# Four PSUM banks instead of two for the up steps of a fused retention and feed-forward kernel, and one pair of terms in another order

## Chip, cores and metric

The kernel runs on one core of one Trainium2 chip. The metric is the device time of one execution in microseconds (us). The span of a profile is about 1.8 us shorter than the time of the same execution.

The profiles name the engines: PE does the matmuls, PEld is its loading of weights, ACT does the gelu, DVE and POOL do elementwise work. POOL also issues most loads, and SP issues the transposes by DMA and the stores.

## The reference

Two stages follow one another. The first is a causal linear attention with decay (retention), 8 batches, 8 heads, 576 positions, head size 64. The second is a feed-forward block on all 4608 tokens.

```python
scores = (q @ k.T) / sqrt(64)                       # per batch and head
ret    = scores * gamma[h] ** (i - j)  (i >= j, else 0)
x      = (ret @ v), heads side by side              # 4608 x 512
h      = x @ w_in                                   # 512 -> 2048
out    = (h * sigmoid(1.702 * h)) @ w_out           # 2048 -> 512
```

## The kernel before

Tokens go in units of 128 rows (36 units) and chunks of 4 units (9 chunks). PSUM has eight banks, by name: H0 and H1 for the feed-forward matmuls, O0 and O1 for the outputs of the attention ("values" and "inter" terms), S0 to S3 for scores and states.

Every feed-forward matmul is issued as two 64-column halves, which run side by side (in the profile they start 3 or 4 ns apart). An "up" step makes one 128 x 512 tile of h in one bank with four such pairs; then ACT takes the bank through the gelu into SBUF. Up steps take turns on H0 and H1:

```python
def mm(y, lhs, rhs, reads, bank, start, stop=True, **kw):
    for r in HALVES:                                   # columns 0-63, 64-127
        op("pe", lambda e, r=r: e.matmul(y[r], lhs[:, r], rhs, ...),
           reads=reads, writes=[bank])
...
def up(c, f):
    bank = f"H{count['up'] % 2}"
    count["up"] += 1
    hb = banks[bank].ap()
    for a in range(HP):                                # 4 pairs of matmuls
        mm(hb, w_in_sb[:, a, P * f : P * f + P], xT[c % 3][:, a, :], [...],
           bank, a == 0, a == HP - 1)
    op("act", lambda e: e.activation(gT[c % 2][:, f, :], hb, AF.Gelu_apprx_sigmoid),
       reads=[bank], writes=[f"gT{c % 2}_{f}"])
```

The recording helper `op` turns these reads and writes into semaphore waits: the first weight load of an up step waits until the gelu that last read its bank has ended.

A phase is 16 up steps of one chunk, or the 16 "down" steps of one chunk. The attention of two coming units (a "block") is played after one step of each phase, in the whole phases after step 13 counted from 0. From the whole phases on only the block uses O0 and O1, until the last down phase; between blocks they lie idle.

```python
def block(m):                       # units a = 2m, b = 2m + 1
    inter(a); inter(b)              # state times q, into O0, O1
    scores(a + 2); scores(b + 2)    # needs the transposed q, k of units a+2, b+2
    scores_out(a + 2, 0)
    values(a); values(b)            # masked scores times v, into O0, O1
    values_out(a); values_out(b)    # DVE: O0, O1 -> xT
    ...
```

Before the first up phase the first four units are worked off one by one (the "head" of the run). For unit 3 the inter term is first, which needs the state that ACT copies for unit 2:

```python
        head_k(2, "act")            # state of unit 2, copied by ACT
        ...
        inter(3)
        values(3)
        values_out(3)
        ...
        play(16, lambda f: up(0, f), {9: [lambda: head_in(4, "dve")], ...})
```

`head_in(4)` transposes k and q of unit 4 on PE after step 9 of the first up phase; it needs their loads.

## Time and profile before

| | before |
|---|---|
| time, median of 3 (range) | 306.97 us (306.8 to 308.05) |
| span of the profile | 305.4 us |
| PE busy | 297.3 us (97%) |
| pace of a pair of 512-column matmuls | 0.216 us |
| an up step: four pairs on PE, one gelu on ACT | 0.8635 us without a loss, 0.597 us |

These lines are from the page of the profile before: engines, the chain that ended last, and groups of instructions (line, engine, operation, output and inputs, shape, count, then busy us, mean ns of one, idle us before it and what ended it).

```profile
span 305.4 us, 8273 instructions
PE 297.3 (97%) x3728; PEld 167.7 (55%) x3728; DVE 131.7 (43%) x277; ACT 121.4 (40%) x214; POOL 113.3 (37%) x139
...
PE 72%; DMA 15%; POOL 12%; issue 1%; DVE 0%; SPq 0%; POOLq 0%
...
L313 PE MATMUL psH<-xT,w_in_sb 128*64 128x512 bf16 (+1 forms) x1280 | 131.0, 359 | 0.1
L456 ACT ACTIVATE gT<-psH 128x512 bf16<-128x512 f32 x128 | 76.5, 597 | 49.6 <-PE psH L313 49.6
L313 PEld LDWEIGHTS psH<-xT,w_in_sb 128*64 128x64 bf16 x1280 | 63.1, 109 | 57.0 <-ACT gT L456 21.6
```

L313 is the helper `mm`, so groups are told apart by their tiles: `psH<-xT,w_in_sb` is an up step, `psH<-w_out_sb,gT` a down step. PE shows 0.1 us of idleness in up steps, and yet the weight loads (PEld) wait 21.6 us for the gelu.

The waits view of before, with the total, how often, and the longest:

```profile
engine line waited for: us in total, times, longest us
PEld psH L313 <- ACT gT L456: 23.5, 78, 0.3
```

Three stretches of the timeline view on PE before (start, duration, instruction, count, and in brackets the idle time before it). They are the end of the head, the wait for unit 4, and the block near 84 us:

```profile
start us, us, engine line op out<-in xcount [idle before <-releaser]
16.48 0.42 PE L432 MATMUL psO<-pm,vp 128*64 128x128 bf16 x8
16.70 0.42 PE L313 MATMUL psO<-qkT,kv 128*64 128x128 bf16 x8
17.53 0.41 PE L313 MATMUL psO<-qkT,kv 128*64 128x128 bf16 x8 [0.41 <-ACT kv L366]
17.78 0.39 PE L432 MATMUL psO<-pm,vp 128*64 128x128 bf16 x8
...
18.95 8.90 PE L313 MATMUL psH<-xT,w_in_sb 128*64 128x512 bf16 x80
...
28.24 0.41 PE L313 MATMUL psS<-ident,kq 128*64 128x128 bf16 x8 [0.16 <-DMA kq<-in_q_dram]
...
83.98 0.40 PE L413 MATMUL psS<-qkT 64*128 64x128 bf16 x8 [0.57 <-DMA qkT<-kq]
84.30 0.64 PE L432 MATMUL psO<-pm,vp 128*64 128x128 bf16 x16
```

At 17.53 us PE waits for ACT before the inter term of unit 3. At 28.24 us it waits for the q load of unit 4, and at 83.98 us for the transposed q and k of unit 13. After that last wait the chain that ended last holds PE alone, but for the last copy of an output on DVE (0.42 us). So the run has two parts: a start that DMA and POOL can hold up, until about 84 us, and some 221 us that only PE's own pace decides. I use the values of the block (84.30 us here, `psO<-pm,vp` x16) as the boundary: 305.36 - 84.30 = 221.06 us lie behind it.

### The profile page before, as it was taken

Reading aid. Unit: us, or ns where it says so; the run is one execution under the profiler, and the core shown is the slowest. Engines: PE = TensorE matmul, PEld = TensorE weight load, DVE = VectorE, ACT = ScalarE, POOL = GpSimd, SP = SyncE. Lnnn points to the kernel's source line nnn. Section 1 sums busy time; section 2 is a strip of 40 time slices with the busy share of each in tenths; the row PEclk is TensorE's granted clock in tenths of the full one; section 3 lists DMA queues with packets and bytes.
Section 4 is the critical chain, followed back from the end, with each engine's and each line's share of the span. In section 5 each row is a group of like instructions: output and inputs, shape, how many; then the busy total and the mean of one; then the engine's idle time right before and its main releaser. Section 6 shows DMA issues by size and latency. Waiting matters only on the chain.

```text
span 305.4 us, 8273 instructions
## 1 busy us (share of the span) xinstructions
PE 297.3 (97%) x3728; PEld 167.7 (55%) x3728; DVE 131.7 (43%) x277; ACT 121.4 (40%) x214; POOL 113.3 (37%) x139
## 2 busy tenths in 40 slices
PE   7789999999999999999999999999999999999996
PEld 3544699556554555455545554555455545554455
DVE  5681860418444464245444554426352635310000
ACT  8566346211146313631363126412651165116611
POOL 9799920745245464260328024600662000000000
PEclk9999999999999999999999999999999999999999
DMA  9999999999997999997699859894989420110022
GB/s 141 194 207 191 188 206 135 143 174 242 122 210 170 131 199 194 131 149 104 133 173 142 103 118 166 155 119 109 173 148 98 105 71 0 36 71 34 2 55 85
DMA packets 118131, 40.65 MB, mean 133 GB/s; under 512 B 107024, under 2 KB 111376, under 8 KB 118096
## 3 DMA queue, kind: packets, MB, share of 16 engines
q0 software_dynamic: 80016, 22.55, 68.4%
q1 hardware_dynamic: 38080, 17.57, 23.9%
q8 instruction: 29, 0.48, 0.7%
q14 instruction: 6, 0.05, 0.1%
HBM read 36.70 MB, written 9.44 MB: 151 GB/s over the span
## 4 chain that ended last, share of the span: by engine, by line
PE 72%; DMA 15%; POOL 12%; issue 1%; DVE 0%; SPq 0%; POOLq 0%
PE psH L313 60%; DMA kq<-in_q_dram 9%; POOL kq L203 6%; PE psS L313 4%; DMA qkT<-kq 3%; POOL vn L217 3%; PE psO L313 3%; PE psO L432 2%; DMA vn<-in_v_dram 2%; PE psS L413 2%; POOL vp L303 1%; POOL w_out_sb L232 1%; POOL w_in_sb L226 0%; POOL iota_c L238 0%; DVE osb L508 0%
## 5 line engine op out<-in xcount | busy, mean ns | idle before, releaser
L313 PE MATMUL psH<-xT,w_in_sb 128*64 128x512 bf16 (+1 forms) x1280 | 131.0, 359 | 0.1
L313 PE MATMUL psH<-w_out_sb,gT 128*64 128x512 bf16 x1024 | 115.5, 379 | 0.0
L456 ACT ACTIVATE gT<-psH 128x512 bf16<-128x512 f32 x128 | 76.5, 597 | 49.6 <-PE psH L313 49.6
L313 PEld LDWEIGHTS psH<-xT,w_in_sb 128*64 128x64 bf16 x1280 | 63.1, 109 | 57.0 <-ACT gT L456 21.6
L313 PEld LDWEIGHTS psH<-w_out_sb,gT 128*64 128x64 bf16 x1024 | 56.1, 110 | 48.6 <-ACT gT L456 1.9
L217 POOL DMA_DIRECT2D vn<-in_v_dram x39 | 33.6, 873 | 115.1 <-DMA qkT<-kq 115.1
L486 ACT ACTIVATE osb<-psH 128x512 f32<-128x512 f32 x32 | 19.1, 597 | 106.7 <-PE psH L313 106.7
L422 DVE TENSOR_TENSOR pm<-psS,mask 128x512 bf16<-128x512 f32 x64 | 41.3, 684 | 44.9 <-PE psS L413 44.9
L203 POOL DMA_DIRECT2D kq<-in_q_dram x39 | 34.4, 888 | 0.0
L203 POOL DMA_DIRECT2D kq<-in_k_dram x39 | 34.2, 883 | 0.0
L442 DVE TENSOR_TENSOR xT<-psO,gq 128x512 bf16<-128x512 f32 x36 | 23.5, 684 | 12.5 <-PE psO L432 12.0
L383 DVE TENSOR_TENSOR kvf<-psS,kvf 64x256 f32<-64x256 f32 x24 | 10.1, 422 | 25.4 <-PE psS L313 25.2
L303 DVE TENSOR_TENSOR vp<-vn,vfac 128x512 bf16<-128x512 f32 x29 | 18.8, 688 | 0.2
L381 DVE COPY kvf<-psS 64x256 f32<-64x256 f32 x12 | 5.1, 422 | 19.8 <-PE psS L313 19.7
L313 PEld LDWEIGHTS psS<-vp,kq 128*64 128x64 bf16 x256 | 10.3, 110 | 5.9 <-ACT kv L366 0.7
L413 PE MATMUL psS<-qkT 64*128 64x128 bf16 x288 | 12.2, 218 | 1.4 <-ACT qkT L338 0.7
L471 ACT ACTIVATE gT<-psH 128x512 bf16<-128x512 f32 x16 | 9.6, 597 | 8.4 <-PE psH L313 8.4
L313 PE MATMUL psS<-vp,kq 128*64 128x128 bf16 x256 | 12.6, 220 | 0.2 <-POOL vp L303 0.2
L508 DVE COPY osb<-psS 128x256 f32<-128x256 f32 x1 | 0.4, 425 | 28.5 <-PE psS L313 28.5
L432 PE MATMUL psO<-pm,vp 128*64 128x128 bf16 x288 | 12.0, 221 | 0.0
L389 DVE TENSOR_TENSOR kv<-psS,kvf 64x256 bf16<-64x256 f32 x12 | 5.1, 422 | 16.2 <-PE psS L313 16.1
L386 DVE CAST kv<-kvf 64x256 bf16<-64x256 f32 x36 | 11.4, 317 | 1.2
(52 smaller groups left out, 132.1 us busy)
## 6 DMA issues: line engine op xcount, KB each, us to landing
vn<-in_v_dram POOLq DMA_DIRECT2D x31, 256.0 KB, 5.3
out_dram<-osb SPq DMA_DIRECT2D x31, 256.0 KB, 2.4
kq<-in_k_dram POOLq DMA_DIRECT2D x31, 128.0 KB, 5.8
kq<-in_q_dram POOLq DMA_DIRECT2D x31, 128.0 KB, 5.9
w_in_sb<-in_moe_w_in_dram POOLq DMA_DIRECT2D x4, 512.0 KB, 9.9
w_out_sb<-in_moe_w_out_dram POOLq DMA_DIRECT2D x4, 512.0 KB, 14.6
out_dram<-osb SPq DMA_DIRECT2D x10, 128.0 KB, 2.4
vn<-in_v_dram POOLq DMA_DIRECT2D x8, 128.0 KB, 3.4
```

The source lines that it names most:

```text
L203: e.dma_start(kq[sl][p0 : p0 + n, i, :].rearrange("p (h d) -> p h d", d=DH), src[b, :, s0 : s0 + n, :].rearrange("h p d -> p h d"),)
L217: e.dma_start(vn[sl][p0 : p0 + n, :, :], v[b, :, s0 : s0 + n, :].rearrange("h p d -> p h d"),)
L303: op(eng, lambda e: e.tensor_tensor(vp[u % NVP].ap(), vn[sl].ap(), vfac[:, ty, :, None].to_broadcast([P, H, DH]), ALU.mult), reads=[f"vn{s ...
L313: op("pe", lambda e, r=r: e.matmul(y[r], lhs[:, r], rhs, start=start, stop=stop, skip_group_check=True, **kw), reads=reads, writes=[bank])
L383: op("dve", lambda e, d=acc, s=src: e.tensor_tensor(d, s, d, ALU.add), reads=[bank, kfk], writes=[kfk])
L386: op("dve", lambda e, d=dst, s=acc: e.tensor_copy(d, s), reads=[kfk, f"kv{kind}_{c}"], writes=[kvk])
L413: op("pe", lambda e, hp=hp, hh=hh, bank=bank: e.matmul(by_pair(bank)[:, hp, :], qt[64 * hh : 64 * hh + 64, hp, :], qt[64 * hh : 64 * hh + ...
L422: op("dve", lambda e: e.tensor_tensor(pm[u % 4][hh].ap(), by_pair(bank), m[:, None, :].to_broadcast([P, HP, P]), ALU.mult), reads=[bank, " ...
L432: op("pe", lambda e, hp=hp, hh=hh: e.matmul(ob[64 * hh : 64 * hh + 64, hp, :], vp[u % NVP][:, 2 * hp + hh, :], pm[u % 4][hh][:, hp, :], st ...
L442: op("dve", lambda e: e.tensor_tensor(xT[ch % 3][:, :, 128 * j : 128 * j + 128], by_pair(bank), gq[:, ty, :, :], ALU.mult), reads=[bank] + ...
L456: op("act", lambda e: e.activation(gT[c % 2][:, f, :], hb, AF.Gelu_apprx_sigmoid), reads=[bank], writes=[f"gT{c % 2}_{f}"])
L486: op("act", lambda e: e.activation(osb[o].ap(), y, AF.Copy), reads=[bank], writes=[f"osb{o}"])
```

## The change

The intent is to use O0 and O1 in the up steps while the attention does not need them, so that a bank's gelu has more time, and to fill PE's hole before the inter term of unit 3 with that unit's values.

```diff
--- before.py
+++ after.py
@@ -443,11 +443,7 @@
                 xT[ch % 3][:, :, 128 * j : 128 * j + 128], by_pair(bank), gq[:, ty, :, :], ALU.mult),
                reads=[bank] + [f"gq{i}_{ty}" for i in range(HP)], writes=[f"xT{ch % 3}_{j}"])
 
-        count = {"up": 0, "y": 0}
-
-        def up(c, f):
-            bank = f"H{count['up'] % 2}"
-            count["up"] += 1
+        def up(c, f, bank):
             hb = banks[bank].ap()
             for a in range(HP):
                 mm(hb, w_in_sb[:, a, P * f : P * f + P], xT[c % 3][:, a, :],
@@ -456,10 +452,8 @@
             op("act", lambda e: e.activation(gT[c % 2][:, f, :], hb, AF.Gelu_apprx_sigmoid),
                reads=[bank], writes=[f"gT{c % 2}_{f}"])
 
-        def up_half(c, i, half):
-
-            bank = f"H{count['up'] % 2}"
-            count["up"] += 1
+        def up_half(c, i, half, bank):
+
             hb = banks[bank].ap().rearrange("p (a b) -> p a b", b=256)
             n = slice(256 * half, 256 * half + 256)
             for j in range(2):
@@ -511,6 +505,10 @@
                 op("sp", lambda e, c0=c0, c1=c1: e.dma_start(
                     out[S * b + s0 : S * b + s0 + n, c0:c1], osb[r][:, c0:c1]),
                    reads=[f"osb{r}_{i}"], writes=[f"out{u}_{i}"], dma=f"d_last{i}")
+
+        def up_bank(i, n):
+
+            return ("H0", "O0", "H1", "O1")[i % 4] if i < n else ("H0", "H1")[i % 2]
 
         def warm(n):
 
@@ -666,8 +664,8 @@
         head_k(2, "act")
         head_v(2)
         setup_gelu()
-        inter(3)
-        values(3)
+        values(3, True)
+        inter(3, False)
         values_out(3)
         head_k(3, "act")
         setup_tail()
@@ -678,7 +676,7 @@
         scale_v(6, "pool")
         scale_v(7, "pool")
         warm(2)
-        play(16, lambda f: up(0, f), {
+        play(16, lambda f: up(0, f, up_bank(f, 8)), {
             9: [lambda: head_in(4, "dve")],
             11: [lambda: head_s(4)],
             12: [lambda: head_in(5, "dve")],
@@ -690,11 +688,11 @@
         warm(1)
         ready_t(4)
         fetch((8, 9), (10, 11), 8)
-        play(8, lambda i: up_half(1, i, 0), {
+        play(8, lambda i: up_half(1, i, 0, up_bank(i, 0)), {
             1: [lambda: head_vs(6)],
             5: [lambda: head_vs(7)],
         })
-        play(8, lambda i: up_half(1, i, 1), {})
+        play(8, lambda i: up_half(1, i, 1, up_bank(i, 8)), {})
         steps = [(down, 0), (down, 1)]
         for c in range(2, NCH):
             steps += [(up, c), (down, c)]
@@ -713,7 +711,7 @@
             events[p + 1, 9] = [lambda m=m: ready_v(m + 2)]
         for p, (step, c) in enumerate(steps[:-1]):
             if step is up:
-                play(16, lambda i: up(c, i), {i: events.get((p, i), []) for i in range(16)})
+                play(16, lambda i: up(c, i, up_bank(i, 12)), {i: events.get((p, i), []) for i in range(16)})
             else:
                 play(16, lambda i: down(c, i, ("H0", "H1")), {i: events.get((p, i), []) for i in range(16)})
         for r in (3, 0, 1):
```

In whole up phases steps 0 to 11 go round four banks and steps 12 to 15 stay on H0 and H1, since the block is played after step 13. In the first up phase it is the first eight steps, and in the half-width phase after it (`up_half`) the second half.

## The prediction

> **What bounds it.** TensorE. The busy line gives PE 297.3 of 305.4 us (97%), granted clock 0.999. From 84 us to the end the chain of waits is PE alone; before that it is POOL issues and DMA (DMA 15%, POOL 12%). In the timeline a pair of 512-column matmuls starts every 216 ns, so an up step of four pairs costs about 865 ns; its gelu takes 597 ns on ACT. So two banks are nearly enough: the waits view charges the gelu 23.5 us of weight-load idleness (78 waits), but mostly hidden. The gelu of step n-2 ends about 0.80 us after step n-1 starts and the weight load follows about 50 ns later. Weight loads that start 26 ns before their matmul cost nothing; one that starts 7 ns before delays the next pair (232 instead of 216 ns).
>
> The Trainium skill, "TensorE: Matmul & The Clock Gate" (queue depths), says TensorE can pull weight loads ahead of running matmuls. The trace agrees: unblocked loads start 214 ns ahead; those behind a bank wait do not.
>
> **What the change does.** No work is removed or added.
> 1. Up steps on four banks: step n waits for the gelu of step n-4, long done. Counting pair gaps of 229-233 ns after 84 us: 5, 6, 5, 5, 5, 5 and 8 in the seven whole up phases, 13-17 ns each, 0.60 us in all. Only the last phase keeps one (two banks in steps 12 to 15, no attention block between), so 0.59 us goes. The one such gap at the start of a down phase stays.
> 2. The first up phase has four such gaps in its first ten steps (0.06 us).
> 3. Unit 3: its inter term waits 0.41 us for the ACT copy of the state (17.53 us). Its values can run in that hole once POOL's scaled values are there (17.12 us), so the bank is done, and the first up step starts, about 0.2 us earlier (18.95 to 18.73).
>
> **Critical path.** Points 2 and 3 are swallowed: at 27.9 us PE waits (0.33 us over its pace) for unit 4's q load, set by POOL issues and DMA; that wait should grow to about 0.6 us. Anything left falls into the wait (0.73 us over pace) for a transposed qkT at 83.2 us, likewise on POOL and DMA. After 84 us no PE wait on a DMA shows and transposes land some 10 us early, so point 1's 0.59 us is real.
>
> The O banks add no wait: values_out (0.69 us on DVE) precedes the first up step on O0 by nearly three PE steps, and the next block comes two steps after the last gelu on O1.
>
> **Predicted:** 306.97 - 0.6 = 306.4 us; 305.6 to 307.3 with the run-to-run spread (306.8 to 308.05 before). Chances: faster by over 2% 0.01, within 2% 0.98, slower 0.01.
>
> **What would show it.** Right: weight-load waits on the gelu fall from 78 to some 25 or fewer; 232 ns gaps vanish from whole up phases, each about 0.08 us shorter; first up step about 0.2 us earlier but the waits near 28 and 83 us longer. Wrong: gaps of 232 ns remaining (cause not the bank), or the waits at 28 and 83 us not growing.
>
> **What would make it wrong.** The loads at 28 and 83 us landing earlier or later (up to 0.7 us either way); an unseen wait for the O banks before the block.

## More of the kernel before

The Trainium skill ("Trainium Kernel Development and Optimization", Performance Expectations) calls matmul busy time a bad metric for how close a kernel is to roofline, because matmuls are pipelined. In this trace, too, busy time misleads: a matmul whose weights come late is only recorded as longer (395 to 400 ns instead of 379), and the stall stays inside the 97%.

The timeline of the weight loads in an up phase, before:

```profile
88.22 0.57 PEld L313 LDWEIGHTS psH<-xT,w_in_sb 128*64 128x64 bf16 x8 [0.29 <-ACT gT L456]
89.10 0.57 PEld L313 LDWEIGHTS psH<-xT,w_in_sb 128*64 128x64 bf16 x8 [0.31 <-ACT gT L456]
```

Each step's eight weight loads come late and in a bunch, released by the gelu. The next view is PE's timeline in the last up phase, which has no block in it:

```profile
274.77 14.14 PE L313 MATMUL psH<-xT,w_in_sb 128*64 128x512 bf16 x128
288.74 7.07 PE L313 MATMUL psS<-w_out_sb,gT 128*64 128x512 bf16 x64
```

From the first matmul of this phase to the first of the next it takes 288.74 - 274.77 = 13.97 us for 16 steps, 0.873 us a step.

## The result, and the profile after

A ratio in this text is that of one kernel's runs to the other kernel's of the same job, with its 95% interval; it is not quite the ratio of the medians quoted beside it. A gap is the time from the start of the second half of one pair of matmuls to the start of the first half of the next pair.

| | before | after |
|---|---|---|
| time, median of 6 (range) | 306.92 us (306.49 to 308.05) | 306.28 us (305.69 to 307.0) |
| ratio, 95% interval | | 0.9977 (0.9955 to 0.9998) |
| span of the profile | 305.36 us | 304.22 us |
| values of the block near 84 us | 84.30 us | 83.90 us |
| from there to the end | 221.06 us | 220.32 us |
| gaps of 226 to 236 ns within up phases, after 84 us | 39 | 1 |

The difference is under 2%; the interval lies just below 1.

The page after:

```profile
span 304.2 us, 8276 instructions
PE 297.0 (98%) x3728; PEld 176.8 (58%) x3728; DVE 131.7 (43%) x277; ACT 121.3 (40%) x214; POOL 113.2 (37%) x139
...
L313 PEld LDWEIGHTS psH<-xT,w_in_sb 128*64 128x64 bf16 x848 | 47.0, 110 | 30.8 <-DVE xT L442 0.7
```

The waits view after:

```profile
PEld psH L313 <- ACT gT L452: 2.5, 8, 0.3
```

The gelu (now L452) holds weight loads 8 times instead of 78, and only two of the 8 are in up steps. In an up phase the loads now come one pair at a time (0.76 us for eight instead of 0.57) and wait for no gelu:

```profile
88.47 0.76 PEld L313 LDWEIGHTS psO<-xT,w_in_sb 128*64 128x64 bf16 x8
89.33 0.76 PEld L313 LDWEIGHTS psH<-xT,w_in_sb 128*64 128x64 bf16 x8
```

PE's timeline after, in the same stretches as before:

```profile
16.77 0.42 PE L432 MATMUL psO<-pm,vp 128*64 128x128 bf16 x8
17.00 0.42 PE L313 MATMUL psO<-qkT,kv 128*64 128x128 bf16 x8
17.56 0.41 PE L432 MATMUL psO<-pm,vp 128*64 128x128 bf16 x8
17.82 0.41 PE L313 MATMUL psO<-qkT,kv 128*64 128x128 bf16 x8
...
19.12 1.05 PE L313 MATMUL psH<-xT,w_in_sb 128*64 128x512 bf16 x8 [0.23 <-DVE maskc L279]
...
28.62 0.41 PE L313 MATMUL psS<-ident,kq 128*64 128x128 bf16 x8 [0.45 <-DMA kq<-in_q_dram]
...
83.35 0.62 PE L413 MATMUL psS<-qkT 64*128 64x128 bf16 x16
83.90 0.64 PE L432 MATMUL psO<-pm,vp 128*64 128x128 bf16 x16
...
273.75 1.03 PE L313 MATMUL psH<-xT,w_in_sb 128*64 128x512 bf16 x8
...
287.59 7.07 PE L313 MATMUL psS<-w_out_sb,gT 128*64 128x512 bf16 x64
```

The last up phase now takes 287.59 - 273.75 = 13.84 us, 0.865 us a step. Of the 1.14 us between the two spans, 0.74 us lie behind the boundary. The other 0.40 us lie ahead of it: the wait of 0.57 us for unit 13 is not there in this profile. Whether that is the change or chance is a question for the experiments.

The wait "DVE maskc" at 19.12 us is a name given by inference. The first up step waits for two things, xT and the first slice of w_in. xT was finished by DVE at 18.97 us and w_in landed at 18.99 us (18.64 us before), so the two were level.

### The profile page after: what moved, and what is told of

It is laid out like the page before. It is cut to its first block, busy times and chain, and to the rows that moved or that the text cites. A ratio compares the mean times of both kernels' runs of the same rounds, so it can differ in the third digit from the quotient of the medians.

```text
span 304.2 us, 8276 instructions
## 1 busy us (share of the span) xinstructions
PE 297.0 (98%) x3728; PEld 176.8 (58%) x3728; DVE 131.7 (43%) x277; ACT 121.3 (40%) x214; POOL 113.2 (37%) x139
## 4 chain that ended last, share of the span: by engine, by line
PE 89%; DMA 6%; POOL 3%; DVE 1%; issue 0%; POOLq 0%
PE psH L313 61%; PE psO L313 17%; PE psS L313 5%; DMA kq<-in_q_dram 3%; PE psS L413 3%; PE psO L432 3%; DMA vn<-in_v_dram 2%; POOL kq L203 2%; POOL vp L303 1%; DVE pm L422 0%; POOL w_in_sb L226 0%; DVE kv L368 0%; DVE qkT L327 0%; DVE xT L442 0%; POOL iota_c L238 0%
## 5 line engine op out<-in xcount | busy, mean ns | idle before, releaser
L313 PE MATMUL psH<-xT,w_in_sb 128*64 128x512 bf16 (+1 forms) x848 | 93.5, 355 | 0.2 <-DVE maskc L279 0.2
L313 PEld LDWEIGHTS psH<-xT,w_in_sb 128*64 128x64 bf16 x848 | 47.0, 110 | 30.8 <-DVE xT L442 0.7
L452 ACT ACTIVATE gT<-psH 128x512 bf16<-128x512 f32 x82 | 49.0, 597 | 35.4 <-PE psH L313 35.2
L313 PE MATMUL psO<-xT,w_in_sb 128*64 128x512 bf16 (+1 forms) x432 | 51.8, 363 | 0.0
L313 PEld LDWEIGHTS psO<-xT,w_in_sb 128*64 128x64 bf16 x432 | 24.6, 110 | 17.1
L452 ACT ACTIVATE gT<-psO 128x512 bf16<-128x512 f32 x46 | 27.5, 597 | 13.6 <-PE psO L313 13.6
L442 DVE TENSOR_TENSOR xT<-psO,gq 128x512 bf16<-128x512 f32 x36 | 23.4, 683 | 11.5 <-PE psO L432 10.9
```

The costliest lines, as they stand in the source:

```text
L313: op("pe", lambda e, r=r: e.matmul(y[r], lhs[:, r], rhs, start=start, stop=stop, skip_group_check=True, **kw), reads=reads, writes=[bank])
L442: op("dve", lambda e: e.tensor_tensor(xT[ch % 3][:, :, 128 * j : 128 * j + 128], by_pair(bank), gq[:, ty, :, :], ALU.mult), reads=[bank] + ...
```

## Experiments

My theory: the gain is the late weight loads in the whole up phases, caused by the wait for the bank's gelu, and it appears in full because nothing but PE decides the time after 84 us. What the change does before 84 us is swallowed by waits for loads. Rivals: the new order for unit 3 carries part of the gain; the number of banks matters beyond the gelu; or the gelu waits were hidden and the gain is chance at the start.

The main reading is the same for all runs: the boundary, and what lies behind it. Here are the 14 profiles together (us; each is one execution; "over pace at 83 us" is the gap of PE's matmul starts ahead of unit 13's scores, less 56 ns, the pace of 128-column pairs):

| kernel | boundary | behind it | over pace at 83 us | time, median | before, same chip |
|---|---|---|---|---|---|
| before | 84.30 | 221.06 | 0.73 | 306.97 | |
| after | 83.90 | 220.32 | none | 306.28 | 306.92 |
| banks_only | 84.51 | 220.32 | 0.62 | 306.44 | 306.77 |
| unit3_only | 83.30 | 221.05 | none | 307.13 | 306.77 |
| three_banks | 83.74 | 220.46 | none | 305.95 | 306.77 |
| after_again | 84.84 | 220.32 | 0.77 | 306.04 | 306.77 |
| unit4_later | 84.02 | 220.33 | 0.52 | 306.30 | 306.85 |
| kq_sooner | 83.42 | 220.31 | none | 306.28 | 306.85 |
| both_waits | 85.25 | 220.33 | none | 305.82 | 306.85 |
| tail_banks | 84.23 | 220.20 | 0.04 | 306.06 | 307.61 |
| long_gelu_two | 83.92 | 223.76 | 0.45 | 309.39 | 306.92 |
| long_gelu_four | 84.69 | 220.75 | 0.87 | 307.08 | 306.92 |
| longer_gelu_two | 83.72 | 229.30 | none | 315.33 | 307.61 |
| longer_gelu_four | 84.42 | 221.64 | 0.30 | 308.02 | 307.61 |

The stretch behind the boundary repeats to 0.02 us from run to run and chip to chip (the five kernels with the change's bank rule read 220.31 to 220.33), while the boundary moves between 83.30 and 85.25 us. (The expectations below speak of the same stretch from a point 0.3 us sooner, the start of unit 13's scores; there it was 221.38 us before and 220.65 us with the change.) So a difference of a tenth of a microsecond can be read from the stretch in one profile, and could not be read from the times, which scatter over more than 1 us.

### banks_only: the banks without unit 3

```diff
-        values(3, True)
-        inter(3, False)
+        inter(3)
+        values(3)
```

> The banks part alone: up steps on four banks, unit 3 in the old order. My theory (the gain is the late weight loads behind a bank wait, and nothing else): the gaps of 229-233 ns in whole up phases after 84 us fall from 39 to about 1, each whole up phase is about 0.08 us shorter, the stretch from the last scores at about 84 us to the end is 0.59 us shorter than before, and the time is the same as with the whole change: 0.6 us under before (ratio about 0.998), whatever the wait at 83 us adds or takes (up to 0.7 us). Rival (the reordering of unit 3 carries a good part of the gain): about 0.2 to 0.4 us of it is missing here.

Measured: 306.44 us, ratio 0.9975 (0.9949 to 1.0). The stretch is 220.32 us, the same as with the whole change, one gap of 232 ns is left, and the gelu holds weight loads 8 times. The banks carry all of the 0.74 us behind the boundary. The size was expected at 0.59 us; it is larger.

### unit3_only: the order of unit 3 without the banks

```diff
-        inter(3)
-        values(3)
+        values(3, True)
+        inter(3, False)
```

> The unit 3 part alone, up steps on two banks as before. My theory (swallowed by the wait for unit 4's q load near 28 us): the first up step starts 0.1 to 0.2 us earlier relative to the values of unit 2, PE's wait near 28 us is longer by as much, and the time is that of before within 0.1 us. Rival (the head is on the path): 0.2 us under before. The gaps of 229-233 ns stay at 39 after 84 us in both.

Measured: 307.13 us against 306.77 us, ratio 0.9997 (0.9974 to 1.0021). The stretch is 221.05 us with 39 gaps, as before. No gain shows; the interval would still hold one or two tenths either way. The part "0.1 to 0.2 us earlier" missed in this run: from the values of unit 2 to the first up step it took 2.71 us against 2.48 us before. In the runs with the new order this distance was 2.25 to 2.35 us five times (after, after_again, kq_sooner, long_gelu_four, longer_gelu_four), which is the expected gain of 0.13 to 0.23 us. In unit3_only and other runs it was longer. three_banks shows such a case in its PE timeline:

```profile
16.17 0.42 PE L432 MATMUL psO<-pm,vp 128*64 128x128 bf16 x8
16.39 0.42 PE L313 MATMUL psO<-qkT,kv 128*64 128x128 bf16 x8
17.68 0.41 PE L432 MATMUL psO<-pm,vp 128*64 128x128 bf16 x8 [0.88 <-POOL vp L303]
17.90 0.42 PE L313 MATMUL psO<-qkT,kv 128*64 128x128 bf16 x8
```

The values of unit 3 waited for the scaled v of POOL, which in turn waits for a load. So the reordering is worth about 0.2 us of PE's time when that load is early. When it is late, it costs about as much (my estimate from the 2.71 and 2.48 us): the inter term, which stood ahead of the values and could run during that wait, now comes behind it. In neither case did the median of the time show it. The wait near 28 us did not grow in unit3_only, though my theory had it grow: it was 0.20 us over pace, against 0.33 us before. So this run does not show the swallowing.

### three_banks: three banks instead of four

```diff
-            return ("H0", "O0", "H1", "O1")[i % 4] if i < n else ("H0", "H1")[i % 2]
+            return ("H0", "O0", "H1")[i % 3] if i < n else ("H0", "H1")[i % 2]
```

> The whole change, but the first twelve up steps take turns on three banks instead of four. My theory (all that matters is that the gelu of the bank was over well before the weight load): step n waits for the gelu of step n-3, which ended some 0.9 us before, so no 229-233 ns gaps and the same time as with four, 0.6 us under before. Rival (the fourth bank is needed, for instance since weight loads can be pulled ahead over more than one step): part of the gaps stay, and up to half of the 0.6 us is lost.

Measured: 305.95 us, ratio 0.9962 (0.9942 to 0.9983), the lowest median of its job, but the stretch is 220.46 us, 0.14 us more than with four. "No gaps" missed: 8 stayed. The cause is in my cycle and not in the number of banks: step 11 falls on H1 and step 13 again, two steps apart, in each of the seven phases (the eighth gap is the one at the end that four banks have too). Seven gaps for 0.14 us is 20 ns each. Steps 0 to 11 on three banks have no gap. What matters is the distance to the bank's last use; three steps are enough.

### after_again: the change on the same chip

> The whole change once more, on the chip of the three others, to compare with: 0.6 us under before. My theory: equal to banks_only and three_banks within 0.2 us. The wait at 83 us, missing in the first profile of the change, is there or not by chance: its size should be the landing of unit 13's transposed q and k less the time at which PE comes to it, between 0 and 0.8 us.

Measured: 306.04 us, ratio 0.9979 (0.9951 to 1.0006); the stretch is again 220.32 us. The wait for unit 13 is back:

```profile
83.51 0.40 PE L413 MATMUL psS<-qkT 64*128 64x128 bf16 x8
84.52 0.40 PE L413 MATMUL psS<-qkT 64*128 64x128 bf16 x8 [0.61 <-DMA qkT<-kq]
```

In this profile the transposed q and k of unit 13 landed at 84.47 us; in the first profile of the change at 82.65 us, and before at 83.93 us. So the 0.40 us ahead of the boundary, in which the first two profiles differ, can't be told from chance: with the same kernel the boundary came 0.94 us later here.

### unit4_later, kq_sooner, both_waits: the two waits at the start

unit4_later (with the change):

```diff
-            9: [lambda: head_in(4, "dve")],
+            10: [lambda: head_in(4, "dve")],
```

> The whole change, with unit 4's transposes one up step later (after the eleventh step instead of the tenth). PE then comes 0.87 us later to the q load it waited for near 28 us. My theory: that wait (0.61 us over pace with the change) goes, PE is about 0.6 us earlier from 30 us on, but the wait for unit 13 at 83 us is longer by what PE gains, unless unit 13 lands early: so no gain on the median of the change (within 0.2 us), and 0.6 us at most in runs where unit 13 lands early. Rival (the head is on the path whatever the loads at 83 us do): 0.6 us under the change on the median, 305.5.

kq_sooner (with the change):

```diff
-            (0, 5): [lambda: ready_t(5), lambda: fetch((10, 11, 12, 13), (12, 13), 10)],
+            (0, 5): [lambda: ready_t(5), lambda: fetch((10, 11), (12, 13), 10), lambda: fetch((12, 13), (), 10)],
```

> The whole change, with the loads of k and q of units 12 and 13 issued ahead of the values of these units (about 1.8 us sooner), unit 4 as in the change. My theory: unit 13's transposed q and k land about 1.5 us sooner (81 to 83 us instead of 82.7 to 84.5), so the wait at 83 us, which was there in four of six profiles with 0.6 to 0.8 us, goes in all runs: the median comes down by 0.3 to 0.5 us against the change and the spread of the runs (over 1 us with the change) narrows. Rival (the spread comes from elsewhere, say from the start of the run): median and spread as with the change.

both_waits has both edits.

> Both edits together. My theory of two waits in a row: with both gone, the 0.6 us that PE gains at 28 us reaches the end, and the time is 0.9 to 1.1 us under the change, near 305.2, and 1.7 us under before. Rival (one of the waits alone carries it): as the better of the two single edits.

Measured: 306.30, 306.28 and 305.82 us, with ratios to before of 0.9989 (0.9961 to 1.0018), 0.9981 (0.9958 to 1.0003) and 0.9973 (0.9950 to 0.9997). Each edit did to its wait what it should: with unit4_later no wait near 28 us shows and the one at 83 us is there (0.52 us over pace), with kq_sooner unit 13 landed at 82.14 us and that wait is gone, and with both neither shows. (The expectation of kq_sooner counts this wait in four of six profiles; by the table it was in three of the six taken until then.) But no gain over the change can be told from chance. kq_sooner's runs spread over 1.5 us, those of the change over 1.3 and 2.1 us, which is what its rival said. The profile of both_waits is of the slowest of its six runs (307.40 us; the others took 305.57 to 306.17 us) and has the latest boundary of all, 85.25 us: its first up step came at 19.91 us instead of 19.12 us, and PE waited 1.8 us in two places for POOL's scaled v, as the waits view of PE from 16 to 85 us shows:

```profile
PE psO L432 <- POOL vp L303: 1.8, 2, 1.5
```

So in this run the 0.6 us at 28 us were not won by taking away these two waits, since loads that landed late made others. Whether the five faster runs won part of it, no profile shows. That head work of PE is swallowed is consistent with unit4_later. It is not shown cleanly, since the times scatter by more than the 0.6 us in question. What decides the landing of the early loads stays open.

### long_gelu_two and long_gelu_four: a longer gelu

Both split each gelu of the whole up steps in two activations of half the columns, the first in the kernel before, the second with the change:

```diff
-            op("act", lambda e: e.activation(gT[c % 2][:, f, :], hb, AF.Gelu_apprx_sigmoid),
-               reads=[bank], writes=[f"gT{c % 2}_{f}"])
+            for z in (slice(0, 256), slice(256, 512)):
+                op("act", lambda e, z=z: e.activation(gT[c % 2][:, f, z], hb[:, z], AF.Gelu_apprx_sigmoid),
+                   reads=[bank], writes=[f"gT{c % 2}_{f}"])
```

> The kernel before (two banks), with each gelu of the whole up steps in two activations of 256 columns. The half-width phase's 512-column gelu takes 597 ns; I expect about 0.38 us for 256 columns, so 0.78 us for a step, still under PE's 0.865 us. My theory (two banks leave PE one step in which the bank's gelu must end): bank free 0.2 us too late in each step, so each whole up step takes about 1.05 us instead of 0.87 and the time is 15 to 24 us longer than before. Rival (PE is bound by its own work, the waits for the gelu are hidden whatever its length so long as ACT keeps up): within 1 us of before.

> The same split gelu in the kernel with the change (four banks). My theory: each step has nearly three steps in which the bank's gelu may end and ACT at 0.78 us a step keeps up with PE's 0.865, so whole up steps stay at 0.865 us but for the last steps of a phase that are back on two banks: 0 to 2 us over the change, under 309. Rival (the activations themselves limit, at their rate): as long as with two banks, over 320.

Measured: 309.39 us (ratio 1.0077) and 307.08 us (1.0002), each of two runs. The direction is that of the theory: behind the boundary two banks lose 2.70 us and four lose 0.43 us. The size for two banks missed by far, because the dose did, and because a step took up only half of it, as the end of this section shows. Two pieces overlap on ACT: the second started 281 ns after the first and took 377 ns, 658 ns instead of 597 in all. The dose was 61 ns and not 200. The Trainium skill ("Perfetto Trace Analysis", Optimizing Scalar/DVE Operations) puts the overhead of one more activation that reads PSUM at about 51 ns of the engine's time; what the profile shows is about twice that, since the half that acknowledges the write overlaps with the next instruction. The run comes near it with 61 ns, and I should have used this. In the last phase an up step rose from 0.873 us to 0.9035 us on average, by half of the dose.

That suggests a loop of two steps: the matmuls of a step, the gelu of its bank, and the weight load of the step after next. In the trace before, from the first matmul of a step to its gelu it is 1.07 us (88.248 to 89.319 us), the gelu takes 0.597 us, the weight load follows 0.05 us later, and it has to come some 0.026 us ahead of its matmul. (In the whole up phases of this trace behind 84 us, a first load 6 or 7 ns ahead left the next gap at 230 to 233 ns, and one 22 to 24 ns ahead at 215 or 216 ns; with 25 ns or more it was 211 to 215 ns.) The sum is 1.745 us for two steps, 0.873 us a step, which is just what the last phase shows; PE's own pace is 0.8635 us.

### longer_gelu_two and longer_gelu_four: the loop tested with a larger dose

```diff
-            for z in (slice(0, 256), slice(256, 512)):
+            for z in (slice(128 * n, 128 * n + 128) for n in range(4)):
```

> The kernel before (two banks), each gelu of the whole up steps in four activations of 128 columns. In the run with two pieces the pieces overlapped (started 281 ns apart, the second took 377 ns: 658 ns instead of 597), so the dose was 61 ns, and a step of the last phase rose from 0.873 to 0.9035 us on average, by half the dose. From that I estimate for four pieces: starts 175 ns apart, about 795 ns in all, a dose of 198 ns. My theory (two banks make a loop of two steps: matmuls of a step, gelu, weight load, so the step is half of the loop, 0.873 plus half the dose): 0.972 us a step, the stretch after 84 us longer than before by 0.099 times some 90 steps, 9 us, the time near 316. Rival (the loss comes from ACT's rate or from the number of its instructions): the same step time with four banks.

> The same four pieces with the change (four banks). My theory: the loop is of four steps and far from binding; ACT needs about 0.8 us a step or less, under PE's 0.8635, so steps stay at 0.8635 us but for those near the end of a phase that are back on two banks; the stretch after 84 us is at most 1.5 us longer than with the change. Rival: about 0.97 us a step, as with two banks.

Measured: 315.33 us (ratio 1.0258) and 308.02 us (1.0020). A gelu in four pieces took 0.785 us, a dose of 188 ns. With two banks the loop gives (1.745 + 0.188) / 2 = 0.967 us a step; in the last phase, but for its first and last step, steps took 1.046 and 0.887 us in turn, 0.9665 us on average. Behind the boundary two banks lose 8.24 us. The weight loads with two banks in the timeline, and then the waits view with two and with four:

```profile
289.70 0.57 PEld L313 LDWEIGHTS psH<-xT,w_in_sb 128*64 128x64 bf16 x8 [0.31 <-ACT gT L457]
290.75 0.57 PEld L313 LDWEIGHTS psH<-xT,w_in_sb 128*64 128x64 bf16 x8 [0.48 <-ACT gT L457]
```

```profile
PEld psH L313 <- ACT gT L457: 35.5, 89, 0.5
PEld psH L313 <- ACT gT L453: 3.8, 8, 0.5
```

With four banks all steps of that phase but the last two took 0.863 or 0.864 us, at the same ACT work. The rivals (ACT's rate, the number of its instructions) fall. The loss of 1.32 us behind the boundary with four banks sits where a bank comes back after two steps: in the last phase in the steps that are back on H0 and H1, and in the six others mostly in the first down step, which takes H0 two steps after its last up step (its first gap is 0.395 us instead of 0.213 us).

### tail_banks: other banks for the last four steps

On top of both_waits:

```diff
-                play(16, lambda i: up(c, i, up_bank(i, 12)), {...})
+                play(16, lambda i: up(c, i, up_bank(i, 16) if c == NCH - 1 or i < 12
+                                      else ("H0", "H1", "H1", "O0")[i - 12]), {...})
```

> A candidate for the best version: the change, with unit 4 one step later and the k and q loads of units 12 and 13 sooner as in both_waits, and other banks at the end of the up phases: the last four steps on H0, H1, H1, O0 (the attention block lies between the two uses of H1, and O0 is free again by the last step), the last phase on four banks throughout. My theory: the one late weight load at the start of each down phase (about 20 ns, six of them) and the last one of the last phase go, so the stretch from the last scores at about 84 us to the end is 220.5 instead of 220.65 us; the time is that of both_waits less 0.1 us, 1.0 us under before, with the spread of the start of the run, which no edit here has taken away. Rival (H1 in two steps running, or O0 after the block, makes a new wait): the stretch is longer than 220.65 us.

Measured: 306.06 us against 307.61 us on this chip, ratio 0.9957 (0.9935 to 0.9978). The stretch is 220.20 us, 0.12 us under the change (from unit 13's scores 220.52 us, where 220.5 was expected), and no gap of about 232 ns is left behind the boundary in up or down steps. It is the fastest of all kernels behind 84 us. That it is faster in time than the change is not shown: the two were not run on the same chip, and the start scatters by more than 0.12 us.

## Why the prediction was right

The time was predicted at 306.4 us and measured at 306.28 us. Point by point:

- *The cause of the loss* held. In 39 of the 112 whole up steps behind the boundary the first weight load, held by the gelu, came only 6 to 10 ns ahead of its matmul; 78 waits fell to 8 (some 25 or fewer were predicted) and 39 gaps to 1, the one foretold. The gaps at the start of down phases stayed, as foretold, until tail_banks took them away.
- *The size of the main term was too small.* "13-17 ns each", 0.59 us in all, measured 0.74 us. I had compared each gap with the pace of a whole pair, 216 ns. The gaps that I had counted run from the second half of a pair to the first half of the next, and those are 212 or 213 ns without a loss. So each late load costs 17 to 20 ns, and the 38 that went make about 0.72 of the 0.74 us.
- *The rest of the time behind 84 us is PE's alone*: held. The stretch is the same to 0.02 us whatever happens ahead of it. (Its "some 10 us early" does not fit the first transposes behind 84 us: in the profile before, that of unit 15 landed 3.4 us ahead of its scores, those from unit 18 on 10.9 us or more.)
- *Unit 3's reordering does not reach the end*: no gain showed in unit3_only. The 0.2 us of PE's time are real when POOL is early (0.13 us in the first profile of the change, where the w_in slice landed just as xT was ready; counted from the start of the profile the first up step came later, at 19.12 instead of 18.95 us). The prediction did not see that POOL's scaled v can be late, which the trace of one run could not show.
- *The waits near 28 and 83 us grow*: the first went from 0.33 to 0.61 us over pace (about 0.6 was predicted). But in part the load itself was later (28.57 instead of 28.20 us), and banks_only shows 0.71 us without the new order, so this is weak evidence. The second was not there in the first profile after, which by the prediction's own test counts as wrong, and back in after_again. It comes and goes with the landing of unit 13. The prediction named such landings as its largest uncertainty, and they are: the median time moved by 0.64 us, where the stretch behind 84 us alone gave 0.74 us and the start scattered by more than the difference. The close hit of the total is therefore partly luck.
- *No new wait for the O banks*: held. No such wait shows in any run.

## What to carry to other kernels

With n banks in turn, a step can't be shorter than one n-th of the loop from its first matmul over the eviction to the first matmul of the next step in the same bank. The runs show this for two banks (0.873, 0.9035 and 0.9665 us a step for three lengths of gelu); with three or four the loop did not bind. Add that loop up from the trace (here 1.745 us for two steps against PE's 1.727 us): an eviction that is shorter than the step is not yet hidden. Three banks were already enough here; the order of banks where two rules meet matters as much as their number. And split a run at its last outside wait: behind it a single profile tells a tenth of a microsecond, which medians of a few whole runs can't.

## What the Trainium skill lacked or had wrong

- "TensorE: Matmul & The Clock Gate" (Architectural detail, queue depths) says that loads of weights can be pulled ahead of running matmuls and that a matmul can begin before its load completes. The runs agree (loads 214 ns ahead where nothing holds them, a matmul recorded 7 ns after the start of a 106 ns load). The page lacks what a late load costs: 25 ns or more ahead cost nothing, 6 or 7 ns ahead cost 17 to 20 ns.
- "Perfetto Trace Analysis" (Optimization Strategy) says that consistent bubbles can mean too little PSUM. Here too little PSUM made hardly any bubble: 0.1 us of PE idleness in up steps while 0.74 us was lost. It showed in the weight loads' waits and in matmuls of 395 to 400 ns instead of 379.
- "Perfetto Trace Analysis" (Optimizing Scalar/DVE Operations) says that breaking up instructions may help where ACT causes bubbles on other engines. It lacks the condition: here the bank is freed as a whole, and breaking up the gelu only made it longer, 597 ns in one piece, 658 in two, 785 in four.
- No page has how loads scatter at the start of a run: the same transposed q and k landed between 82.05 and 84.47 us in the runs here, and PE's wait for them was between nothing and 0.87 us over its pace, where the change gained 0.74 us.
